# A one-layer transformer block whose last attention groups of each chunk are normalized on the spot by TensorE transposes, with inverse sums and LayerNorm roots from one GpSimd power each

## The chip, the cores and the metric

One core of one Trainium2 chip. The metric is the device time of one execution in microseconds; smaller is better. The kernel before was timed three times: 883.87, 884.46 and 886.01 us, median 884.46 us.

## The reference

A pre-norm transformer block on x of 2048 tokens and 640 features: 32 heads of 20 features, then a gated MLP of width 1728. Weights and data are bfloat16.

```python
def _A_ref(x, wqkv, wo):                       # S = 2048, D = 640, H = 32, Dh = 20
    qkv = (x @ wqkv).reshape(B, S, 3, H, Dh).transpose(2, 0, 3, 1, 4)
    q, k, v = qkv[0], qkv[1], qkv[2]
    scores = jnp.einsum("bhqd,bhkd->bhqk", q, k) * (Dh ** -0.5)
    o = jnp.einsum("bhqk,bhkd->bhqd", _softmax(scores, axis=-1), v)
    return o.transpose(0, 2, 1, 3).reshape(B, S, D) @ wo

h = x + _A_ref(_layernorm(x), A_wqkv, A_wo)
g, u = hn @ w_gate, hn @ w_up                  # hn = _layernorm(h)
out = h + (gelu(g) * u) @ w_down
```

## The kernel before

**Planner.** The program is written as a list of operations, each with an engine, an assumed duration, a priority and its dependencies (class Sched, `op`). `schedule` (line 98) plays that list through once when the program is built and fixes, for each of the five engines, one order of instructions; `emit` (line 263) writes these orders with semaphore waits. Nothing is reordered on the chip: each engine takes its instructions in that order, and a wait holds everything behind it on its engine. A smaller priority number goes first. When PE would be idle, the planner puts in filler matmuls on kt_all and on a zero tile (lines 187 to 227), which compute nothing that is used.

**Tiling.** The 2048 query tokens are cut into eight chunks of 512, 256, 256, 256, 256, 256, 128 and 128 (SIZES). The heads form eight groups of four. A slot is as many groups of one chunk as make 512 columns, so there are 32 slots: eight for chunk 0, four for each of chunks 1 to 5, two for chunks 6 and 7. A slot has 64 score tiles of 128 keys by 512 columns.

**Scores and probabilities.** `unit` issues the score matmuls of two or three tiles (line 976) into PSUM banks 0 to 2 or 3 and 4, and one ACT exponential over 1024 or 1536 columns writes the probabilities to a ring (tiles pts, and pts2 inside rege). D_SLOT says how many quads of tiles per slot do not go to ACT: `d_exp` computes them on VectorE (an eviction at line 889, then four integer operations as terms of an approximate exponential). `pv_op` multiplies the probabilities with the values and a column of ones into bank 6, so that row 20 of each head's 32 rows holds the sum of exponentials.

**Normalization.** At a slot's end `epilogue` copies bank 6 to osb. In chunks 0 to 6 it then calls `spread`: the sums go to DRAM and come back as 128x16 (rc), GpSimd inverts them by a bit trick and three Newton steps (ten operations on rn and rc), the inverses go to DRAM and are broadcast to 128 partitions (bsum), VectorE multiplies (on16), and the rows go to DRAM (attn). All of these transfers are issued on SP. Only chunk 7, the last, is normalized without DRAM: four transposes of osb (line 1063), a reciprocal (line 1069) and scalings into o_nat (line 1072).

**The background work.** After the last slot of a chunk, `post` loads that chunk's attention rows from DRAM into oT, does the output projection (chain, line 676 in 32-column pieces or 681) with the residual (line 1124), LayerNorm (`ln_stats`, `ln_rsqrt`, `ln_apply`), transposes the rows by DMA (for chunk 7 on PE, line 622), and runs gate, up and down matmuls (lines 676 and 1158; 676 and 1223). `ln_rsqrt` computes the root on GpSimd by a bit trick and two Newton steps in 14 operations, then a VectorE reciprocal. This work fills PE between the scores of the next chunk's slots. The width 1728 is cut into 14 tiles of 128 features, the last of which overlaps its neighbour.

**The prologue.** LayerNorm of x, transposes, key, query and value projections. A bound of each score's size is made from the largest absolute key per feature (ka, kd, sel) and added to the queries, so the exponentials cannot overflow. The first scores wait for that bound of head group 0 (`proj_k`, `q_bound0`, lines 793 and 797).

Of the kernel before, what the change touches and what calls it, by code (L numbers as in the profile page):

```python
# [8 lines left out]
ALU = mybir.AluOpType  # L9
# [9 lines left out]
DRAIN = {"pe": 0.165, "act": 0.115, "dve": 0.085, "pool": 0.05, "sp": 0.0}  # L19
WARM_WIN, WARM_MIN = 3.4, 0.5  # L20
PAD_WIN, PAD_MIN = 3.4, 0.42
QK_LEAD = .65
PE_AGE = 3.5
SD_AGE = 0.6
SD_ROW = 0
# [24 lines left out]
class Sched:  # L50
# [47 lines left out]
    def schedule(self):  # L98
# [22 lines left out]
        due = None  # L121
        total = len(ops)
        scores = sum(o.eng == "pe" and o.mode == "row" for o in ops)
        while done < total:
            assert events, "no operation can start"
            t = heapq.heappop(events)
            while events and events[0] <= t + 1e-9:
                heapq.heappop(events)
            for e in ENGINES:
# [8 lines left out]
                while ready[e]:  # L138
# [18 lines left out]
                    if got and 0 < p[0] < 1 and scores > 1 and t - o.ready < (  # L157
                            SD_AGE if mode[e] != "row" else SD_ROW if row_end[o.rows[0]] > max([row_start + 0.01] + [freed[b] for b in got]) + 0.02 else 0):
                        skipped.append((p, i))
                        continue  # L160
# [7 lines left out]
                    if chosen is None:  # L168
                        chosen, banks = o, got
                        if e != "pe" or p[0] < 1 or o.mode == mode[e] or t - o.ready > PE_AGE:  # L170
                            break
# [39 lines left out]
                scores -= o.eng == "pe" and o.mode == "row"  # L211
                if e == "pe" and self.pad is not None and o.tag and o.tag[0] in ("O", "Oq"):
# [21 lines left out]
                if e == "act":  # L234
                    due = t + o.dur + (0.905 if o.dur > 1.2 else 1.332) - QK_LEAD if o.mode == "exp" else None
# [7 lines left out]
                o.fin = t + o.dur + o.lat  # L243
                heapq.heappush(events, free[e])
# [16 lines left out]
        self.span = max(o.fin for o in ops)  # L261
# [63 lines left out]
S = 2048  # L325
# [11 lines left out]
F0 = tuple(min(128 * f, DFF - 128) for f in range(NF))  # L337
SCALE = DH ** -0.5
# [9 lines left out]
PV_QUADS = 2  # L348
PR, PR2 = 12, 4
D_SLOT = (0,) + (3,) * 27 + (2, 3, 2, 1)  # L350
SUMS = (0,) + (1,) * 6 + (0, 1, 1, 0) + (1,) * 5 + (2,) + (1,) * 10 + (0, 1, 1, 1, 0)
# [4 lines left out]
VN = 6  # L356
D_RING = (6,) * 26 + (4, 6, 12, 12, 0, 6)
D_FIRST, D_SPAN = 0, 18
# [5 lines left out]
P_EV = 1.8  # L364
P_QK, P_PV, P_TAIL, P_PRO, P_EPI, P_LN, P_BG = 0, 1, 1.2, 1.5, 2, 2.5, 3
P_KQ = 3
P_ON = 2.4
V_ACT = (0, 1)
XN_DVE = (9, 13, 15)
V0 = 0  # L370
# [3 lines left out]
def bass_sequential_preLN__mha_block__glu_gated_geglu__prompt_kernel(  # L374
# [12 lines left out]
    with ExitStack() as es:  # L387
# [21 lines left out]
        identf = sb("identf", [128, 128], FP32)  # L409
# [13 lines left out]
        kd = sb("kd", [128, NA], FP32)  # L423
        kt_all = sb("kt_all", [128, NG, S])
# [9 lines left out]
        o_nat = sb("o_nat", [128, 1, D])  # L434
# [41 lines left out]
        ob = carve(2 * D).rearrange("p (i s) -> p i s", i=2)  # L476
        I16 = mybir.dt.int16
        ka = carve(2048)
        pts2 = carve(PR2 * 512)
        qreg = [qt_all[:, c, :, :].rearrange("p g s -> p (g s)") for c in range(2)]  # L480
        d_any = [(carve(2048).bitcast(I16), ("da", 0))]
        d_early = [(ha_f[:, 2048 * i:2048 * i + 2048].bitcast(I16), ("dh", i)) for i in range(3)]
# [32 lines left out]
        cst(I("memset", zer[:], 0.0), "zer", 32)  # L515
        op("act", I("activation", nm[:, 0:1], zer[:, 0:2].bitcast(FP32), ACT.Sqrt), 1.5, P_QK, reads=["zer"], writes=["nm0"])
# [21 lines left out]
        for j in range(4):  # L538
            cst(I("memset", off0[32 * j:32 * j + 1, :], OFF), "off0", 1)
        cst(I("memset", identf[:], 0.0), "identf")  # L540
        cst(I("affine_select", out=identf[:], in_=identf[:], compare_op=ALU.not_equal, fill=1.0,
              base=0, pattern=[[-1, 128]], channel_multiplier=1), "identf")
# [36 lines left out]
        def ln_rsqrt(t0, n, prio, table=False, sqrt=False):  # L579
# [7 lines left out]
            d = v if table or sqrt else lambda fn, r, w: op(POOL, fn, 0.285, prio, reads=r, writes=w)  # L587
# [7 lines left out]
            if table:  # L595
                op("act", I("activation", sd16[:, t0:t0 + n], sd16[:, t0:t0 + n], ACT.Sqrt), 0.2, -1, mode="sqrt", reads=[ks],
                   writes=[ks])
                v(I("reciprocal", y, sd16[:, t0:t0 + n]), [ks], rk)
                return
# [724 lines left out]
```

## Time and profile before

| | |
|---|---|
| median of three runs | 884.46 us |
| profiled execution, its own time | 884.74 us |
| its span, first to last instruction | 883.0 us |
| PE, DVE, ACT, POOL busy | 830.0, 753.4, 832.0, 134.2 us |
| first exponential starts, last one ends | 37.02, 842.06 us |
| granted TensorE clock | 1.00 in every stage |

PE is TensorE's matmuls and PEld its weight loads, DVE is VectorE, ACT is ScalarE, POOL is GpSimd, and SP issues DMAs. In the views, "out<-in" gives tile names; rege and regw are two large regions that hold many tiles one after another, so that a name like rege<-ps can mean several things, which the line number tells apart: many operations share line 395. Matmuls that work on separate 32-column or 32-row parts of the array overlap, four to a group, so a row "x60" of such matmuls is 15 groups. PE's busy time counts overlapping matmuls once. In the chain of waits a piece reads start, length, engine and line, and the count of instructions merged in it.

### The profile page before, as it was taken

Reading aid. Unit: us, or ns where it says so; the run is one execution under the profiler, and the core shown is the slowest. Engines: PE = TensorE matmul, PEld = TensorE weight load, DVE = VectorE, ACT = ScalarE, POOL = GpSimd, SP = SyncE. Lnnn points to the kernel's source line nnn. Section 1 sums busy time; section 2 is a strip of 40 time slices with the busy share of each in tenths; the row PEclk is TensorE's granted clock in tenths of the full one; section 3 lists DMA queues with packets and bytes.
Section 4 is the critical chain, followed back from the end, with each engine's and each line's share of the span. In section 5 each row is a group of like instructions: output and inputs, shape, how many; then the busy total and the mean of one; then the engine's idle time right before and its main releaser. Section 6 shows DMA issues by size and latency. Waiting matters only on the chain.

```text
span 883.0 us, 36651 instructions
## 1 busy us (share of the span) xinstructions
PE 830.0 (94%) x16658; PEld 405.4 (46%) x16658; DVE 753.4 (85%) x1356; ACT 832.0 (94%) x798; POOL 134.2 (15%) x431
## 2 busy tenths in 40 slices
PE   3999999999989899999999999999999999999998
PEld 1532222222234333344545555545554556666687
DVE  8839999999879889788899878999899997976864
ACT  6799999999999999999999999999999999999931
POOL 5001111110201201111031211113101321120200
PEclk9999999999999999999999999999999999999999
DMA  7211130332264410001121101101020101103000
GB/s 268 75 44 58 31 79 19 107 90 68 76 175 126 106 30 19 19 8 42 42 64 35 33 17 50 34 8 35 27 57 20 30 19 42 45 16 65 6 17 24
DMA packets 57298, 46.95 MB, mean 53 GB/s; under 512 B 25524, under 2 KB 50704, under 8 KB 57144
## 3 DMA queue, kind: packets, MB, share of 16 engines
q1 hardware_dynamic: 57144, 44.62, 19.2%
q8 instruction: 130, 2.13, 1.0%
q14 instruction: 24, 0.20, 0.1%
HBM read 30.68 MB, written 11.04 MB: 47 GB/s over the span
## 4 chain that ended last, share of the span: by engine, by line
ACT 56%; PE 28%; DVE 12%; POOL 1%; issue 1%; DMA 1%
ACT pts L395 44%; ACT rege L395 12%; PE ps L676 9%; PE ps L976 7%; PE ps L395 5%; PE ps L681 4%; DVE qt_all L395 3%; DVE rege L889 2%; PE ps L1158 2%; DVE rege L395 2%; DVE qt_all L889 1%; DVE stats L395 1%; PE ps L1223 1%; DMA rege<-xn_t 1%; ACT qt_all L395 1%
## 5 line engine op out<-in xcount | busy, mean ns | idle before, releaser
L395 ACT ACTIVATE pts<-ps 128x1024 bf16<-128x1024 f32 (+1 forms) x585 | 639.3, 1244 | 8.0 <-PE ps L976 6.1
L976 PE MATMUL ps<-qt_all,kt_all 32*128 32x256 bf16 (+2 forms) x4096 | 301.2, 272 | 24.3 <-ACT pts L395 17.5
L976 PEld LDWEIGHTS ps<-qt_all,kt_all 32*128 32x128 bf16 x4096 | 101.8, 92 | 227.1 <-ACT pts L395 150.5
L395 ACT ACTIVATE rege<-ps 128x1536 bf16<-128x1536 f32 (+1 forms) x129 | 178.6, 1401 | 1.7 <-PE ps L395 1.5
L889 DVE TENSOR_SCALAR rege<-ps 128x512 int16<-128x512 f32 x220 | 148.7, 682 | 27.9 <-PE ps L976 27.2
L676 PE MATMUL ps<-rege,regw 128*32 128x256 bf16 (+1 forms) x3360 | 152.4, 292 | 5.7 <-ACT rege L395 1.8
L395 PE MATMUL ps<-pts,v_all 128*21 128x256 bf16 (+2 forms) x2711 | 132.1, 273 | 0.3 <-ACT pts L395 0.2
L395 PE MATMUL ps<-rege,v_all 128*21 128x256 bf16 (+2 forms) x1877 | 130.1, 287 | 2.3 <-issue 1.5
L889 DVE TENSOR_SCALAR qt_all<-ps 128x512 int16<-128x512 f32 x136 | 92.2, 683 | 19.7 <-PE ps L976 18.8
L676 PEld LDWEIGHTS ps<-rege,regw 128*32 128x32 bf16 x3360 | 77.9, 96 | 44.5 <-issue 24.9
L395 DVE TENSOR_SCALAR rege<-rege 128x2048 int16<-128x2048 int16 x139 | 93.3, 684 | 2.5 <-PE ps L395 1.9
L681 PE MATMUL ps<-regw 128*128 128x512 bf16 (+1 forms) x360 | 90.2, 356 | 2.5 <-ACT regw L628 2.0
L395 POOL TENSOR_SCALAR rn<-rc 128x16 int32<-128x16 int32 x30 | 8.6, 288 | 526.2 <-DMA rc<-sums 525.8
L395 PEld LDWEIGHTS ps<-pts,v_all 128*21 128x21 bf16 x2711 | 62.4, 91 | 30.1 <-issue 23.3
L676 PE MATMUL ps<-regw,rege 128*32 128x320 bf16 x1568 | 74.7, 301 | 0.6 <-DVE rege L889 0.5
L395 DVE TENSOR_SCALAR qt_all<-qt_all 128x2048 int16<-128x2048 int16 (+2 forms) x118 | 68.8, 594 | 0.6
L395 PEld LDWEIGHTS ps<-rege,v_all 128*21 128x21 bf16 x1877 | 50.1, 91 | 36.4 <-issue 20.9
L395 PE MATMUL ps<-qt_all,v_all 128*21 128x256 bf16 (+1 forms) x1360 | 58.8, 262 | 0.5 <-DVE qt_all L395 0.3
L395 DVE TENSOR_SCALAR qt_all<-rege 128x2048 int16<-128x2048 int16 x83 | 56.2, 689 | 1.6 <-PE ps L395 1.0
L681 PEld LDWEIGHTS ps<-regw 128*128 128x128 bf16 x360 | 29.3, 99 | 51.1 <-issue 26.6
L1211 DVE TENSOR_TENSOR rege<-rege,ps 128x512 bf16<-128x512 bf16 (+1 forms) x53 | 35.8, 677 | 12.1 <-PE ps L676 11.2
L676 PEld LDWEIGHTS ps<-regw,rege 128*32 128x32 bf16 x1568 | 36.6, 96 | 19.0 <-issue 9.3
(113 smaller groups left out, 724.2 us busy)
## 6 DMA issues: line engine op xcount, KB each, us to landing
bsum<-rsums SPq DMA_DIRECT2D x120, 64.0 KB, 2.1
rege<-in_A_x_dram SPq DMA_DIRECT2D x5, 640.0 KB, 5.6
q_rows<-regw SPq DMA_DIRECT2D x20, 128.0 KB, 1.8
out_dram<-rege SPq DMA_DIRECT2D x16, 160.0 KB, 2.6
attn<-on SPq DMA_DIRECT2D x120, 20.0 KB
regw<-in_B_w_gate_dram SPq DMA_DIRECT2D x5, 432.0 KB, 3.6
regw<-in_B_w_up_dram SPq DMA_DIRECT2D x5, 432.0 KB, 3.3
kt_all<-k_rows SPq DMA_DIRECT2D x12, 160.0 KB
```

The lines of the kernel that those rows point to most:

```text
L395: return lambda eng: getattr(eng, method)(*args, **kwargs)
L676: return [lambda eng, j=j: eng.matmul(out()[32 * j:32 * j + 32], l[:, 32 * j:32 * j + 32], r, start=start, stop=stop, tile_position=(0, 32 ...
L681: fn = col4(lambda: bank(bk, n), l, r, k == 0, k == len(steps) - 1) if col else lambda eng, l=l, r=r, k=k: eng.matmul(bank(bk, n), l, r, s ...
L889: d_ops.append(op("dve", lambda eng: eng.tensor_scalar(v[:, 512 * h:512 * h + 512], bank(b), EXP_MUL, -32000.0, ALU.mult, ALU.max), c_dve( ...
L976: return lambda eng: eng.matmul(out()[:, kk * nq:(kk + 1) * nq], kt_all[32 * j:32 * j + 32, g, kt * 128:(kt + 1) * 128], qt_all[32 * j:32 ...
L1158: lambda eng, a=a, f=f, fi=fi: eng.matmul(bank(bk)[:, fi * nq:(fi + 1) * nq], w[:, a, F0[f]:F0[f] + 128], hnT[:, a, 128 * tb:128 * tb + nq ...
L1211: hdone.append(op("dve", lambda eng, bu=bu, fv=fv, w=w: eng.tensor_tensor(fv, fv, bank(bu, w), ALU.mult), c_dve(w), p, reads=[ku] + hkeys( ...
L1223: f == NF - 1) if nq >= COL else lambda eng, f=f, o=o, hf=hf, bk=bk: eng.matmul(
```

## The change

1. *Direct normalization.* In chunks 0 to 6 the last slot (in chunk 0 the last two) is no longer sent through `spread`. Four TensorE transposes, a VectorE reciprocal and scalings put the normalized rows in a small buffer (wda or sq), and small 32-column matmuls with the identity turn them back into oT. The oT load from DRAM carries only the other slots' rows, in two DMAs.
2. *Powers.* The inverse of the sums is one GpSimd power with exponent -1, the LayerNorm root one power with exponent 0.5.
3. *Prologue.* The largest absolute key of head group 0 is reduced by VectorE with an absolute-value reduction (three of four from SBUF, the last one from PSUM). Values wait for it from the fourth tile on.
4. *Last feature tile.* 1728 = 13 x 128 + 64. Where the chunk has 256 or 512 tokens, the last tile's 64 features are laid out as two halves of the tokens, so these matmuls stream half the columns; a second copy of the last w_down rows (wda) serves the first half.
5. *Output.* The last addition is written over h_sb instead of a separate buffer.
6. *Planner.* Several constants become tuples by slot, background work gets new priorities, PV matmuls go in one quad at a time (PV_QUADS 2 to 1), the probability ring grows from 16 to 19 tiles, D_SLOT, SUMS, D_RING and D_SPAN change by slot, chunk 3's LayerNorm rows are transposed on PE (XP_PE), and ACT's assumed pace gets 12 ns per instruction more.

```diff
-DRAIN = {"pe": 0.165, "act": 0.115, "dve": 0.085, "pool": 0.05, "sp": 0.0}
+DRAIN = {"pe": 0.165, "act": 0.118, "dve": 0.085, "pool": 0.05, "sp": 0.0}
-QK_LEAD = .65
-PE_AGE = 3.5
+QK_LEAD = (0.65, 0.55,) + (0.65,) * 4 + (0.72, 0.72, 0.6,) + (0.72,) * 8 + (0.6, 0.6, 0.72, 0.6,) + (0.68,) * 11
+ACT_GAP = .012
+PE_AGE = (2.5,) * 9 + (1.5, 2.5, 2.5, 5.0,) + (1.0,) * 7 + (5.0,) + (1.0,) * 5 + (3.5, 2.0, 2.0, 1.0, 3.5, 1.0,)
...
-PV_QUADS = 2
-PR, PR2 = 12, 4
-D_SLOT = (0,) + (3,) * 27 + (2, 3, 2, 1)
+PV_QUADS = 1
+PR, PR2 = 13, 6
+D_SLOT = (0,) + (3,) * 3 + (2,) + (3,) * 3 + (4,) + (3,) * 19 + (2, 3, 0, 1,)
...
-P_EV = 1.8
+P_EV = 1.5
-P_KQ = 3
+P_KQ = (2, 3, 3, 3)
+X_LAT = 3.0
+O_LAT = 3.2
+XP_PE = (3,)
+P_NOW = 0.9
+PW = 0.4
+P_K0 = 1.0
+P_DV = 0.5
+P_ADD = 0.6
+P_ST = 0.7
+P_OUT = 2.5
...
@@ ln_rsqrt @@
+            if not dve:
+                op(POOL, I("tensor_tensor", sd16[:, t0:t0 + n], sd16[:, t0:t0 + n], rn[:, 1, 0:n], ALU.pow), PW, prio,
+                   reads=[ks, "pwc"], writes=[ks])
                 v(I("reciprocal", y, sd16[:, t0:t0 + n]), [ks], rk)
                 return
...
@@ proj_qk @@
+            if dkey[0] == "ku" and t == 0:
+                red = lambda src, r: op("dve", lambda eng: eng.tensor_reduce(km[:, c:c + 1], src(), AX.X, ALU.max, apply_absolute_value=True),
+                                        0.62, P_K0, reads=[r], writes=[("km", c)])
+                m = [red(lambda: bank(bk), key)] if c == 3 else []
...
@@ spread @@
-            x, y, z = rc[:, s, :], rn[:, 0, :], rn[:, 1, :]
-            d = lambda fn, r, w: op(POOL, fn, 0.285, P_EPI, reads=r, writes=w)
-            d(I("tensor_scalar", y.bitcast(I32), x.bitcast(I32), -1.0, RECIP_MAGIC, ALU.mult, ALU.add), [("rc", s)], ["ry"])
-            for i in range(3):
-                d(I("tensor_tensor", z, x, y, ALU.mult), [("rc", s), "ry"], ["rz"])
-                d(I("tensor_scalar", z, z, -1.0, 2.0, ALU.mult, ALU.add), ["rz"], ["rz"])
-                d(I("tensor_tensor", x if i == 2 else y, y, z, ALU.mult), ["ry", "rz"], [("rc", s) if i == 2 else "ry"])
+            op(POOL, I("tensor_tensor", rc[:, s, :], rc[:, s, :], rn[:, 0, :], ALU.pow), PW, P_EPI, reads=[("rc", s), "pwc"],
+               writes=[("rc", s)])
...
@@ epilogue @@
-            if c < len(CHUNKS) - 1:
+            tail = c == len(CHUNKS) - 1
+            g_dir = [g for ss, (cc, gg) in enumerate(slots) if cc == c and (tail or gg[-1] == NG - 1 or c == 0 and gg[0] == NG - 2)
+                     for g in gg]
+            if gs[0] not in g_dir:
                 spread(s, c, gs, nq)
                 return
...
+            op("sp", I("dma_start", oT[:, 0:na, tok], src[0:128 * na, :].rearrange("(a p) s -> p a s", p=128)), 0.4, P_EPI,
+               reads=ars, writes=hk, sem=f"oT{c}", lat=O_LAT + nq * 0.004, after=tuple(e_ops) if c == 0 else ())
+            op("sp", I("dma_start", oT[0:pf, na, tok], src[128 * na:f0, :]), 0.4, P_EPI,
+               reads=ars, writes=hk, sem=f"oT{c}", lat=O_LAT + nq * 0.004, after=tuple(e_ops) if c == 0 else ())
...
+                        fs = [lambda eng, i=i, a=a, tt=tt, q=q, b3=b3: eng.matmul(
+                            bank(b3)[q:q + 32, i * nq + tt * 128:i * nq + tt * 128 + 128],
+                            buf[:, tt, 128 * a + q - f0:128 * a + q - f0 + 32], ident[:], start=True, stop=True,
+                            tile_position=(0, q), skip_group_check=True) for q in range(p0, 128, 32)]
+                        op("pe", fs, 0.057, P_NOW, mode="col", util=0.03, reads=[okey(0, tt), "ident"], writes=[k3],
+                           acq=[b3] if i == 0 and tt == 0 else [], after=free if i == 0 and tt == 0 else ())
...
@@ post @@
-            if not tail:
-                op("sp", I("dma_start", oT[:, :, 128 * tb:128 * tb + nq],
-                           adr[c].rearrange("g j e s -> (g j e) s").rearrange("(a p) s -> p a s", p=128)), 0.4, P_EPI,
-                   reads=[("adr", c, gs[0], j) for cc, gs in slots if cc == c for j in range(4)],
-                   writes=[("hnT", tt) for tt in range(tb, tb + nt)], sem=f"oT{c}", lat=4.5 + nq * 0.002, after=first)
...
+                    half = nq >= COL and f == NF - 1
...
+                        fn = [lambda eng, a=a, fi=fi, j=j: eng.matmul(
+                            bank(bk)[32 * j:32 * j + 32, fi * nq:fi * nq + nq // 2], w[:, a, FL + 32 * (j % 2):FL + 32 * (j % 2) + 32],
+                            hnT[:, a, 128 * tb + j // 2 * (nq // 2):128 * tb + (j // 2 + 1) * (nq // 2)], start=a == 0, stop=a == NA - 1,
+                            tile_position=(0, 32 * j), skip_group_check=True) for j in range(4)] if half else col4(lambda fi=fi: bank(bk)[:, fi * nq:(fi + 1) * nq], w[:, a, F0[f]:F0[f] + 128],
```

220 lines of the change are left out of this document (144 added, 76 removed).

## The prediction

> **What bounds the kernel now.** I read the page's totals and chain of waits first, then busy time by stage, then the order in time around the first exponential, one chunk's end, and the end of the run.
>
> ```profile
> span 883.0 us, 36651 instructions
> ACT 56%; PE 28%; DVE 12%; POOL 1%; issue 1%; DMA 1%
> ACT pts L395 44%; ACT rege L395 12%; PE ps L676 9%; PE ps L976 7%; PE ps L395 5%; PE ps L681 4%; DVE qt_all L395 3%; DVE rege L889 2%; PE ps L1158 2%; DVE rege L395 2%; DVE qt_all L889 1%; DVE stats L395 1%; PE ps L1223 1%; DMA rege<-xn_t 1%; ACT qt_all L395 1%
> ```
>
> More than half of the chain is ACT writing probabilities (pts, and the rege copies of that ring). PE follows with background work (L676 is MLP and output projection). One engine does not bound everything, so I split the span where the first exponential starts and the last one ends (us, then busy time of PE, PEld, DVE, ACT, POOL with instruction counts, clock, DMA share, GB/s):
>
> ```profile
> 0.00:37.00 37.00, 22.08 (x154) 12.34 (x154) 30.51 (x96) 24.60 (x45) 12.17 (x32) 1.00 0.52 176
> 37.00:212.00 175.00, 171.43 (x1458) 51.35 (x1457) 148.29 (x261) 173.85 (x161) 19.67 (x60) 1.00 0.24 64
> 212.00:305.00 93.00, 84.81 (x1409) 32.16 (x1405) 80.83 (x142) 93.00 (x87) 15.89 (x55) 1.00 0.45 121
> 305.00:730.00 425.00, 406.74 (x9224) 204.62 (x9228) 383.21 (x647) 423.77 (x394) 70.97 (x226) 1.00 0.13 31
> 730.00:842.00 112.00, 107.44 (x3734) 73.39 (x3726) 87.68 (x161) 108.14 (x102) 15.52 (x58) 1.00 0.16 35
> 842.00:883.00 41.00, 37.53 (x704) 31.51 (x695) 22.83 (x52) 8.61 (x14) 0.00 (x0) 1.00 0.05 18
> ```
>
> Three stages with three limits. Up to 37 us a prologue; from 37 to 842 ACT is busy 173.85 + 93.00 + 423.77 + 108.14 = 798.76 of 805 us, so 6.2 us idle; from 842 on ACT is done and PE is busy 37.53 of 41 us. That last stage is what the change can shorten most, so I ask what PE does there (start, us, work):
>
> ```profile
> 840.10 0.33 PE ps L976 x4
> 840.98 1.42 PE ps L676 x50
> ...
> 849.93 6.77 PE ps L676 x196
> ...
> 861.22 6.90 PE ps L1158 x119
> 868.12 3.81 PE ps L1223 x28
> 871.92 3.75 PE ps L1158 x67
> ...
> 875.70 0.43 DVE rege L1183
> ...
> 876.18 3.99 PE ps L1223 x28
> ```
>
> At 840.10 the last score matmuls run; PE then works almost without a break to 880.17, 40 us. L676 there is chunk 5's MLP, half of L1158 and the first L1223 are chunk 6's: a backlog. The last chunk's own chain queues behind it. Why the backlog exists shows at a chunk's end: its last sums are copied, and the output projection (wo) starts only when sums, inverses, broadcasts and rows have gone through DRAM:
>
> ```profile
> 730.19 0.69 DVE L395 COPY osb<-ps 128x512 f32<-128x512 f32 x1 [1.45 <-PE ps L395]
> 750.66 0.68 DVE L395 TENSOR_TENSOR on<-osb,bsum 128x512 bf16<-128x512 f32 x1
> 763.44 1.09 PE L676 MATMUL ps<-wo,rege 128*32 128x320 bf16 x20
> 831.09 0.27 POOL L395 CAST mv<-mv 128x2 bf16<-128x2 f32 x1 [37.29 <-DVE mv L395]
> 836.36 0.19 POOL L395 TENSOR_TENSOR sd<-nw,rs 128x1 bf16<-128x1 f32 x1
> ```
>
> Chunk 5: 33 us from copy to projection. The last two rows are the ends of chunk 6's root on GpSimd, 14 operations in 5.5 us.
>
> **The change part by part.** Counts come from the two programs' instruction orders; durations from rows.
>
> *Tail.* After the last score matmul the old order holds 140 matmuls of 32x256, 224 of 32x320, 280 of 128x128, 56 of 128x320. The new one holds no 32x256 and no 32x320, 210 of 128x128, 56 of 128x320 and 20 fillers. Moved into the exponential stage: 35 groups of four at 1.42/12.5 = 0.114 us, 56 groups at 6.77/49 = 0.138 us and 70 singles at 6.90/119 = 0.058 us: 4.0 + 7.7 + 4.1 = 15.8 us. What remains on PE is about 24 us, less than the last chunk's own chain, so that chain now ends the run:
>
> ```profile
> 841.39 0.67 ACT L395 ACTIVATE pts<-ps 128x512 bf16<-128x512 f32 x1
> 842.85 0.68 DVE L395 COPY osb<-ps 128x512 f32<-128x512 f32 x1
> 845.34 0.66 PE L1063 MATMUL ps<-identf,osb 128*128 128x128 f32 x4
> 852.66 0.45 DVE L395 TENSOR_SCALAR xn_t<-rege,mu,rs 128x640 bf16<-128x640 bf16 x1
> 856.63 0.45 PE L622 MATMUL ps<-ident,xn_t 128*128 128x128 bf16 x5
> 857.12 0.70 ACT L628 ACTIVATE rege<-ps 128x640 bf16<-128x640 bf16 x1 [3.35 <-PE ps L622]
> 880.19 0.49 DVE L1228 TENSOR_TENSOR rege<-ps,rege 128x320 bf16<-128x320 f32 x1 [1.34 <-PE ps L1223]
> ```
>
> From the last exponential's end (842.06) to the copy 0.8. From copy to the end of xn_t 853.11 - 842.85 = 10.3, less 1.6 that the transposes waited behind L676 (copy over at 843.53, transposes at 845.34), plus 1.1 for two DVE multiplies (0.69 and 0.42, a 512 and a 256 wide L1211) that the new order puts into it: 9.8. Transposes and their eviction, 856.63 to 857.82, and a step: 1.4. Gate and up, 140 x 0.058 = 8.1; the last multiply 0.5; down 4.0; 880.19 to the end 2.8. Sum 27.4, against 883.0 - 842.06 = 40.9: 13.5 us less. The two multiplies may find their place elsewhere: 14.6 at best; if the two waits on PE stay as now, 13.5 - 1.6 - 3.5 (853.11 to 856.63) = 8.4.
>
> *First exponential.* The abs and maximum steps on key projections become reductions straight from PSUM.
>
> ```profile
> 31.55 0.60 ACT L708 ACTIVATE regw<-ps 128x512 bf16<-128x512 f32 x1 [0.48 <-PE ps L681]
> 34.67 0.24 DVE L395 TENSOR_SCALAR sel<-sel,kd 128x4 bf16<-128x4 bf16 x1
> 34.97 0.39 PE L793 MATMUL ps<-regw,sel 128*128 128x512 bf16 x1
> 37.02 1.45 ACT L395 ACTIVATE pts<-ps 128x1536 bf16<-128x1536 f32 x1 [3.58 <-PE ps L976]
> ```
>
> From the last key eviction to sel now takes 3.1 us; one reduction of 512 (a 512-wide DVE read of PSUM is 0.68, the copy above), a small one and sel make 1.2. But PE, in its fixed order, still has other projections ahead of L793: in all 25 instead of 30 V matmuls of 320 come before the first scores. So the gain is what PE drops, 5 x 0.138 = 0.7 plus some of a short wait: 0.9, between 0 and the 1.9 of the DVE chain.
>
> *ACT's work.* D_SLOT gives 2 quads (8 tiles) back to ACT: two-bank exponentials 448 to 443, three-bank 265 to 271. Their pitch, from the chain:
>
> ```profile
> 96.03 5.01 ACT pts L395 x5
> 101.03 1.34 ACT rege L395
> ```
>
> Five rows of which one is three-bank: (5.01 - 1.34)/4 = 0.917, and 1.34. So 6 x 1.34 - 5 x 0.917 = +3.5. By the same rows 512 columns cost 0.42. Shorter GELUs (the last feature tile is now half) drop 896 columns, 0.7; one 1024-wide tanh, about one two-bank step, moves out of the tail into the stage, +0.9: +3.7 in all. The planner's other new constants (ACT_GAP, QK_LEAD, PE_AGE, SD_AGE by slot) only set the order, which the counts hold already.
>
> *PE in the stage.* In: 15.8 us, and 1 us of small transposes and 32-wide matmuls per boundary, 6-7. Out: the halved last feature tile, 40 groups of 256 columns and 10 of 512 at half their length, 40 x 0.057 + 10 x 0.114 = 3.4; fillers (matmuls on kt_all and zer, with no use but activity) from 114 groups of 512 columns to 69, 45 x 0.228 = 10.3. Net about +9 in 805 us. What makes room is the time at the boundaries: chunk 5's and 6's projection can start about 25 us earlier. So I let ACT's idle time stay at 6.2 us; bounds: all of it goes (-6.2), or all moved work comes back as ACT waiting (+15.8).
>
> *GpSimd.* 30 chains of ten operations become 22 single powers, and the roots shrink from 14 to 4 operations. No row shows a power. The nearest, a two-operand 128x16 operation, is 0.35; the far end is a whole chain:
>
> ```profile
> L395 POOL TENSOR_TENSOR rn<-rc,rn 128x16 f32<-128x16 f32 x90 | 31.6, 352 | 6.7
> 711.78 1.09 POOL L395 TENSOR_SCALAR rn<-rc 128x16 int32<-128x16 int32 x1 [16.76 <-DMA rc<-sums]
> 718.09 0.22 POOL L395 TENSOR_TENSOR rc<-rn 128x16 f32<-128x16 f32 x1
> DVE rs L395 <- POOL sd L395: 1.5, 4, 0.4
> ```
>
> 0.35 to 6.5 us; I take 0.35, same engine, shape and operands. At that, POOL stays off the path. The last row is the wait that the power lengthens if slow: DVE's reciprocal, with score evictions (L889) behind it in DVE's queue and the gate matmuls behind the normalised rows in PE's.
>
> *The rest at no cost.* Eight slots skip the DRAM trip (82 of 519 SP transfers go; attn rows now move for 22 slots), the oT load is split in two on SP and waits for earlier slots only; DVE trades eight 0.68 multiplies and eight score evictions of the same length for reciprocals, small scalings and evictions, no more work than before, covered by ACT. A weight copy (wda) and a late identity load on idle POOL and SP. If DVE's cover fails, the new evictions delay the projection, not ACT.
>
> *A rule against it.* The clock column above reads 1.00 in every stage. The Trainium skill, "TensorE: Matmul & The Clock Gate", Part 1, says that PE falls to half its clock after an idle window of about 3.4 us; this change removes 45 filler groups. No row here shows such a fall.
>
> **The sum.** -0.9 + 3.7 - 13.5 + 0 = -10.7 against the profiled execution's own 884.74 (span 883.0 and 1.7 around it); the median, 884.46, is 0.3 below it. 884.46 - 10.7 = 873.8.
>
> **The rivals.**
> - *More:* ACT's idle time goes too, and the tail gives 14.6: 873.8 - 6.2 - 1.1 = 866.5. For it: shorter boundary chains; against: ACT has been idle under 1% anyway. 0.13.
> - *The backlog comes back as ACT waiting.* PE is busy 107.44 of 112 us from 730 on, and takes more work in. Fully: 873.8 + 15.8 = 889.6; half: 881.7; slower than before from 10.7/15.8 = 68% on. Against: fillers and a 25 us earlier start. 0.10.
> - *The power is slow* (the other side): place, the seven roots. PE's order is fixed and was laid out for a short root; each microsecond over 0.4 holds the gate matmuls and the scores behind them, up to seven times. It decides from 10.7/7 + 0.4 = 1.9 us; at 3 us, half a chain, 7 x 2.6 = 18.2: 892.0. For: unshown operation. Against: the old root shown took 5.5 us where 13 steps of 0.285 were planned, and PE lived with it. 0.09.
> - *PE clock falls* between 212 and 305, where fillers lie thickest (44 groups, 10 us): 84.81 - 10 = 75 us of work at half speed is 150, +57 over the 93: 931. Against: real work replaces the fillers. 0.02. (This is what the rule of the Trainium skill above would do.)
>
> **How the numbers follow.** Forecast 0.66 (its own range 867 to 880: tail 8.4 to 14.6, start 0 to 1.9, a few us of idle time), rivals 0.13, 0.10, 0.09, 0.02. The range 862 to 885 takes in "more" with room, half of the second rival, and leaves the slow power and the clock out. About 0.3% (2.7 us) is what a measurement of this kernel can tell from no change. Faster: 0.65 + 0.13 + 0.05 = 0.83; same: 0.01 + 0.02 + 0.02 = 0.05; slower: 0.03 + 0.07 + 0.02 = 0.12.
>
> **What would show it.** Right: first exponential near 36 us; last one near 845; then about 27 us in which PE has gaps and no 32-row matmuls; wo within 10 us of a chunk's last copy; a power row of 0.3 to 0.6 us. Wrong: ACT idle above 15 us between (backlog), gaps of PE ending at POOL or at rs (power), a clock under 1.00, or a tail still above 35 us.

## The result, and the profile after

The changed kernel takes 880.24 us (median of five runs, 876.74 to 881.07) against 884.28 us for the kernel before on the same chip: a ratio of 0.994, interval 0.992 to 0.996. Run once more beside the last experiment it took 878.52 us, ratio 0.9925 (0.9912 to 0.9939). It is faster, as forecast, but by 4.0 us in the first series and 7.4 us in the second, where 10.7 us were forecast. The profiled execution of the first series (881.07 us) has a span of 879.4 us; its totals and its chain of waits:

```profile
span 879.4 us, 36235 instructions
PE 839.4 (95%) x16663; PEld 409.0 (47%) x16663; DVE 749.1 (85%) x1369; ACT 839.7 (95%) x800; POOL 94.3 (11%) x85
PE 49%; ACT 30%; DVE 14%; DMA 4%; issue 1%; POOL 1%; SPq 1%; DVEq 0%
```

ACT held 56% of the chain before and PE 28%; now PE holds 49%. (A name that ends in q is that engine's sequencer.) The busy time by stage, in the same columns as before:

```profile
37.00:212.00 175.00, 171.25 (x1406) 51.98 (x1405) 144.35 (x252) 174.61 (x161) 18.63 (x7) 1.00 0.24 63
212.00:305.00 93.00, 89.44 (x1474) 36.28 (x1475) 86.05 (x156) 89.66 (x84) 10.31 (x8) 1.00 0.39 99
305.00:730.00 425.00, 415.71 (x9503) 211.62 (x9502) 391.74 (x676) 422.15 (x390) 48.14 (x29) 1.00 0.12 31
730.00:845.00 115.00, 111.26 (x3680) 72.86 (x3676) 79.38 (x157) 112.30 (x103) 5.33 (x9) 1.00 0.10 24
```

PE is busy 787.7 of these 808 us; before it was 770.4 of 805. ACT's busy time here adds up to 798.72 of 808 us, so 9.3 us idle; before it was 6.2. The clock stays at 1.00. The end of the run in order of time (some of its rows):

```profile
850.65 1.50 ACT L428 ACTIVATE rege<-ps 128x1024 bf16<-128x1024 f32 x2
852.66 0.69 DVE L428 COPY osb<-ps 128x512 f32<-128x512 f32 x1
861.45 0.45 DVE L428 TENSOR_SCALAR xn_t<-rege,mu,rs 128x640 bf16<-128x640 bf16 x1
862.06 0.44 PE L660 MATMUL ps<-ident,xn_t 128*128 128x128 bf16 x5
863.70 7.98 PE L1243 MATMUL ps<-rege,regw 128*128 128x128 bf16 x140
872.19 3.98 PE L1311 MATMUL ps<-regw,rege 128*128 128x320 bf16 x28 [0.52 <-DVE rege L1269]
876.21 0.49 DVE L1316 TENSOR_TENSOR rege<-ps,rege 128x320 bf16<-128x320 f32 x1 [1.41 <-PE ps L1311]
```

The first row merges the last two exponentials, which end at 852.15 (850.65 + 1.50); the tail after them is 27.25 us (879.4 - 852.15), where 27.4 were forecast. No 32-row MLP matmul is left in it. The first exponential starts at 35.97, where about 36.1 was forecast. So the whole miss lies between the two: the exponential stage takes 816.2 us, where 805.0 + 3.7 = 808.7 was forecast.

**Where the stage's time went.** From now on three numbers describe a run: the stage (first exponential's start to last one's end), the tail (from there to the end of the span) and the waits. The waits are a sum over all exponentials of two or three banks: from its start to the start of ACT's next instruction, less the shortest such pitch, which is 0.903 us for two banks and 1.330 us for three. It is 19.0 us before and 26.5 us after; the difference, 7.6 us before rounding, is the miss. ACT's idle time in the view above grew by only 3.1 us, because an exponential's record is longer than the step to the next one's start (1.06 us for two banks, whose shortest step is 0.903): a wait shorter than that overlap leaves no idle time.

```profile
L428 ACT ACTIVATE pts<-ps 128x1024 bf16<-128x1024 f32 x294 | 301.9, 1061 | 1.9 <-PE ps L1026 1.5
```

Sorted by size, waits of 20 to 640 ns, nearly all of them ended by score matmuls (L976, now L1026), grew from 12.1 us to 19.2 us. The few above 640 ns were 4.7 us (four) and are 4.2 us (two). So the growth as a whole is in many short waits for scores, while among the long ones a new one has taken the place of others. That new one is 3.06 us (some rows of the time around it):

```profile
255.81 5.54 ACT L428 ACTIVATE pts<-ps 128x1024 bf16<-128x1024 f32 x5
262.32 0.39 PE L428 MATMUL ps<-kt_all 128*128 128x512 bf16 x1
262.43 0.68 DVE L428 TENSOR_SCALAR rege<-qt_all 128x2048 int16<-128x2048 int16 x1
263.34 0.40 PE L428 MATMUL ps<-kt_all,zer 128*32 128x512 bf16 x4
263.57 0.61 PE L428 MATMUL ps<-rege,v_all 128*21 128x256 bf16 x16
264.23 1.94 ACT L428 ACTIVATE rege<-ps 128x1024 bf16<-128x1024 f32 x2 [2.89 <-PE ps L428]
```

The busy time between 255 and 264 us, in the columns of the stages:

```profile
255.00:264.00 9.00, 8.27 (x163) 3.67 (x159) 8.94 (x15) 6.34 (x6) 1.62 (x2) 1.00 0.33 94
```

ACT stops at 261.34 and waits 2.89 us for a PV matmul that frees its place in the probability ring. That PV comes in PE's fixed order after PV matmuls on VectorE's approximate tiles, and VectorE is busy 8.94 of 9.00 us: this is slot 8, where D_SLOT gives VectorE four quads instead of three, and where VectorE also evicts chunk 0's directly normalized rows (L1160, at 257.66 and 259.29). PE is not what is short here, since it runs fillers (kt_all, zer) in the gap.

The other term is the power. In all groups of GpSimd's operations, it stands with its real price:

```profile
L428 POOL TENSOR_TENSOR rc<-rc,rn 128x16 f32<-128x16 f32 x22 | 68.7, 3124 | 406.9 <-DMA rc<-sums 406.9
L428 POOL TENSOR_TENSOR sd<-sd,rn 128x2 bf16<-128x2 bf16 (+2 forms) x7 | 6.6, 944 | 0.0
```

It takes 3.12 us for the sums and 0.94 us for the roots, where the prediction took 0.35 and the planner (PW) 0.4. The old ten operations took 4.12 us from first to last, as a mean over the 30 slots. Around 300 us the chain of waits runs through two powers and the DRAM trips behind them (start, length, piece):

```profile
297.62 3.66 DMA rc<-sums
301.36 3.44 POOL rc L428
304.82 2.29 DMA rsums<-rc
308.42 2.88 DMA bsum<-rsums
311.40 0.69 DVE on L428
...
318.62 3.29 POOL rc L428
321.94 1.38 DMA rsums<-rc
324.63 3.58 DMA bsum<-rsums
328.23 0.69 DVE on L428
330.72 0.40 PE ps L428 x8
331.92 1.45 ACT pts L428
```

VectorE stands in its fixed order at "on", the multiply with bsum, until the broadcast lands; PE and then ACT (1.15 us of waiting ahead of 331.92) come after it.

### The profile page after: what moved, and what is told of

Read it like the earlier page. It is cut to its first block, busy times and chain, and to the rows that moved or that the text cites. A ratio compares the mean times of both kernels' runs of the same rounds, so it can differ in the third digit from the quotient of the medians.

```text
span 879.4 us, 36235 instructions
## 1 busy us (share of the span) xinstructions
PE 839.4 (95%) x16663; PEld 409.0 (47%) x16663; DVE 749.1 (85%) x1369; ACT 839.7 (95%) x800; POOL 94.3 (11%) x85
## 4 chain that ended last, share of the span: by engine, by line
PE 49%; ACT 30%; DVE 14%; DMA 4%; issue 1%; POOL 1%; SPq 1%; DVEq 0%
ACT pts L428 20%; PE ps L1026 15%; PE ps L719 12%; PE ps L428 12%; ACT rege L428 9%; PE ps L724 6%; DVE qt_all L428 3%; DVE rege L428 2%; DVE rege L939 2%; PE ps L1243 2%; DVE qt_all L939 2%; DMA regw<-in_A_wqkv_dram 1%; PE ps L1311 1%; SPq L428 1%; POOL rc L428 1%
## 5 line engine op out<-in xcount | busy, mean ns | idle before, releaser
L428 ACT ACTIVATE pts<-ps 128x1536 bf16<-128x1536 f32 (+1 forms) x494 | 557.0, 1233 | 5.4 <-PE ps L1026 4.5
L1026 PE MATMUL ps<-qt_all,kt_all 32*128 32x256 bf16 (+2 forms) x4096 | 316.7, 272 | 9.1 <-ACT pts L428 3.3
L428 ACT ACTIVATE rege<-ps 128x1024 bf16<-128x1024 f32 (+2 forms) x221 | 249.1, 1193 | 4.9 <-PE ps L428 2.9
L1026 PEld LDWEIGHTS ps<-qt_all,kt_all 32*128 32x128 bf16 x4096 | 109.0, 92 | 206.8 <-issue 75.7
L719 PE MATMUL ps<-rege,regw 128*32 128x256 bf16 (+1 forms) x3120 | 146.1, 292 | 4.4 <-DVE rege L939 1.1
L428 PE MATMUL ps<-pts,v_all 128*21 128x256 bf16 (+2 forms) x2392 | 142.1, 274 | 0.9 <-DVE osb L428 0.9
L428 PE MATMUL ps<-rege,v_all 128*21 128x256 bf16 (+2 forms) x2204 | 136.9, 285 | 1.9 <-issue 0.6
L428 POOL TENSOR_TENSOR rc<-rc,rn 128x16 f32<-128x16 f32 x22 | 68.7, 3124 | 406.9 <-DMA rc<-sums 406.9
L428 PEld LDWEIGHTS ps<-pts,v_all 128*21 128x21 bf16 x2392 | 49.7, 90 | 48.1 <-issue 40.7
L1297 DVE TENSOR_TENSOR rege<-rege,ps 128x512 bf16<-128x512 bf16 (+2 forms) x53 | 34.8, 657 | 8.8 <-PE ps L719 7.6
```

The costliest lines, as they stand in the source:

```text
L428: return lambda eng: getattr(eng, method)(*args, **kwargs)
L719: return [lambda eng, j=j: eng.matmul(out()[32 * j:32 * j + 32], l[:, 32 * j:32 * j + 32], r, start=start, stop=stop, tile_position=(0, 32 ...
L1026: return lambda eng: eng.matmul(out()[:, kk * nq:(kk + 1) * nq], kt_all[32 * j:32 * j + 32, g, kt * 128:(kt + 1) * 128], qt_all[32 * j:32 ...
L1297: hdone.append(op("dve", lambda eng, bu=bu, fv=fv, w=w: eng.tensor_tensor(fv, fv, bank(bu, w), ALU.mult), c_dve(w), p, reads=[ku] + hkeys( ...
```

## The experiments

All runs by the three numbers; ratios are to the kernel before on the same chip. Stage, tail and waits are of the profiled execution; two profiles of the changed kernel differ by 2 us in the stage.

```
run                              median   ratio [95%]              stage  tail  waits
before                           884.28   1                        805.0  40.9  19.0
changed                          880.24   0.994  [0.992, 0.996]    816.2  27.3  26.5
e12 changed again                878.52   0.9925 [0.9912, 0.9939]  814.1  27.2  24.5
e1  multiply for power           877.64   0.9904 [0.9887, 0.9922]  813.3  27.3  23.6
e2  three powers                 934.72   1.0552 [1.0513, 1.0592]  875.9  27.2  86.3
e9  control: new order           886.75   1.0016 [1.0007, 1.0026]  823.0  28.8  33.4
e3  slot 8: three quads          886.89   1.0006 [0.9992, 1.002]   814.0  34.6  23.5
e4  two quads of PV              886.40   1.0005 [0.9994, 1.0016]  818.1  31.5  29.4
e5  rows through DRAM            889.75   1.0051 [1.0037, 1.0065]  820.8  33.9  32.0
e6  full last tile               891.03   1.0071 [1.0056, 1.0086]  822.6  31.4  33.1
e7  true power price             882.50   0.9968 [0.9957, 0.9979]  813.9  31.3  25.2
e8  before with powers           889.92   1.0062 [1.0042, 1.0082]  812.1  40.1  26.0
e10 before, powers, same order   883.80   0.9988 [0.9976, 1.0]     805.0  40.9  19.0
e11 true price, new constants    874.56   0.9873 [0.9857, 0.9889]  810.8  27.0  21.1
```

**The power's price in a fixed order.** Two runs keep every engine's order and change only what GpSimd issues in it.

```diff
-op(POOL, I("tensor_tensor", rc[:, s, :], rc[:, s, :], rn[:, 0, :], ALU.pow), PW, P_EPI, ...
+op(POOL, I("tensor_tensor", rc[:, s, :], rc[:, s, :], zer[:].bitcast(FP32), ALU.mult), PW, P_EPI, ...
...
-op(POOL, I("tensor_tensor", sd16[:, t0:t0 + n], sd16[:, t0:t0 + n], rn[:, 1, 0:n], ALU.pow), PW, prio, ...
+op(POOL, I("tensor_tensor", sd16[:, t0:t0 + n], sd16[:, t0:t0 + n], rn[:, 1, 0:n], ALU.mult), PW, prio, ...
```

> The changed kernel's order of instructions on every engine, but each GpSimd power is a plain multiply of the same shape (the sums by zero, the roots by 0.5): inverse sums and roots are left out, so 22 slots' attention rows are zero. The power rows should fall from 3.12 us and about 1.0 us to some 0.35 us. Power theory (the seven missing microseconds are waits behind 3.12 us powers in an order laid out for 0.4): the last exponential moves from 850.6 us towards 844.8, the total from 880.2 to about 873 to 875. Slot-8 theory (one fixed stall of 3.06 us at 260 us) and full-PE theory (TensorE has no room in the exponential stage): last exponential within 1.5 us of 850.6, the 3.06 us stall still at 260, total 878.5 to 880.5.

```diff
-op(POOL, I("tensor_tensor", rc[:, s, :], rc[:, s, :], rn[:, 0, :], ALU.pow), PW, P_EPI, ...
+op(POOL, [I("tensor_tensor", pwx[:, i, :], rc[:, s, :], rn[:, 0, :], ALU.pow) for i in (0, 1)] + [
+    I("tensor_tensor", rc[:, s, :], rc[:, s, :], rn[:, 0, :], ALU.pow)], PW, P_EPI, ...
```

> The same order again, with three powers in place of one for each of the 22 inverse sums (two go to a scratch tile): 3.12 us becomes about 9.4 us per slot. Power theory: if 2.7 us too much per power cost 7 us in all, 6.2 us more cost at least another 10: total above 890. Slot-8 and full-PE theories: below 2 us more, about 880 to 882, since the sums' way through DRAM has time to spare.

The GpSimd row of e1:

```profile
L428 POOL TENSOR_TENSOR rc<-rc,zer 128x16 f32<-128x16 f32 x22 | 6.5, 295 | 447.3 <-DMA rc<-sums 447.3
```

From each run's waits, the row in which SP, whose queue issues the DMAs, waits for the inverse sums (us in total, times, longest), for e1, then the changed kernel, then e2:

```profile
SPq L428 <- POOL rc L428: 33.4, 18, 4.1
```

```profile
SPq L428 <- POOL rc L428: 86.6, 21, 6.3
```

```profile
SPq L428 <- POOL rc L428: 221.6, 22, 13.4
```

And e2 in order of time, SP's and PE's instructions around one of these waits:

```profile
140.73 0.34 SPq L428 DMA_DIRECT2D rsums<-rc  x1
144.79 0.59 SPq L428 DMA_DIRECT2D qt_all<-bounds  x1
...
146.87 0.61 PE L1027 MATMUL ps<-qt_all,kt_all 32*128 32x512 bf16 x2 [4.16 <-DMA qt_all<-bounds]
```

A multiply of 0.30 us in the power's place takes 2.9 us off the waits of the first series' profile and 0.9 off the second's; by the ratios (0.9904 against 0.994 and 0.9925) it is worth 2 to 3 us, with intervals that touch that of the first series and overlap that of the second. 877.64 us lies between what the power theory and the two others expected. So the price costs about 1 to 3 of the 7.6 us, near what can be told from nothing, and not all of it; the 3.04 us wait in slot 8 is still there in e1. But the price is not off the path: at 9.4 us the run is 54 us longer, a part of which is a granted clock of 0.965 on average (see the last section). These rows show the way: SP issues in order, the inverse's DMA (rsums) holds the transfers behind it, and at 146.87 the scores have waited 4.16 us for query bounds that were issued late. The slot-8 and full-PE theories, which expected less than 2 us more, fail on e2.

**The control.** Every other edit lays the order out anew, so one run measures what a new order alone costs.

```diff
-D_LAT = 0.3
+D_LAT = 0.31
```

> A control: the changed kernel with one assumed latency of the planner moved from 0.30 to 0.31 us (D_LAT, how early a VectorE tile's scores are placed before its slot needs them); the same instructions and counts, but every order is laid out anew. It tells what a new order alone costs, against which the edits of one constant or one part are to be read. Tuned-order theory (the constants by slot fit this one order, and any other is worse): 3 to 9 us above 880.2, with waits spread over many places, so that most of what three quads, two quads, rows through DRAM and the full last tile lost is the new order and not the edit. Edit theory (those losses are the edits' own): 880 to 882.

The same instructions in a new order cost 0.76% (1.0016 against 0.994), some 6.7 us, as the theory expected by which the constants by slot fit one order. It is one new order; how far others spread was not measured. The 3.09 us wait of slot 8 is there too, and others of 2.45 and 1.32 us are new. So e3 to e7 are read against 1.0016 as well as against the changed kernel.

**Slot 8 with three quads.**

```diff
-D_SLOT = (0,) + (3,) * 3 + (2,) + (3,) * 3 + (4,) + (3,) * 19 + (2, 3, 0, 1,)
+D_SLOT = (0,) + (3,) * 3 + (2,) + (3,) * 3 + (3,) + (3,) * 19 + (2, 3, 0, 1,)
```

> D_SLOT of slot 8 from 4 quads back to 3, order laid out anew. Slot-8 theory: four quads (16 tiles) make VectorE late in that slot, PV matmuls in their fixed order wait for its last tile, and ACT waits for a ring slot. With 3 the 3.06 us stall at 260 falls under 0.5 us, ACT gets four tiles more (4 x 0.42 = 1.7 us), and the last exponential moves by -3.06 + 1.7 = -1.4 to about 849. Full-PE theory: the stall also goes, but what TensorE did in it is now missing, so it comes back as other waits or as a longer tail: total 880 or more, up to 885. Power theory: the stall stays.

The wait is gone (no wait above 0.5 us between 250 and 280), and the stage is 814.0 us: 2.2 less than in the first profile, and the same as in e12. But the tail is 34.6 us. What PE does in it:

```profile
855.76 1.52 PE L724 MATMUL ps<-wo,rege 128*128 128x320 bf16 x10
859.87 3.91 PE L1243 MATMUL ps<-rege,regw 128*128 128x128 bf16 x67 [2.58 <-DVE rege L428]
864.75 3.98 PE L1311 MATMUL ps<-regw,rege 128*128 128x320 bf16 x28 [0.52 <-DVE rege L1297]
868.56 7.98 PE L1243 MATMUL ps<-rege,regw 128*128 128x128 bf16 x140
877.06 3.98 PE L1311 MATMUL ps<-regw,rege 128*128 128x320 bf16 x28 [0.52 <-DVE rege L1269]
```

67 gate and up matmuls and 28 down matmuls of chunk 6 stand behind the last chunk's projection and before its own 140. So without the fourth quad the wait does not arise, and taking it away alone gains nothing: the order that results leaves chunk 6 for the tail. But the quad is not the whole cause, as e5 and e11 below show.

**Two quads of PV at a time.** PV rows' busy time in the stage is 334 us after against 321 before, for no more matmuls, and PV_QUADS went from 2 to 1.

```diff
-PV_QUADS = 1
+PV_QUADS = 2
```

> PV_QUADS from 1 back to 2: PV matmuls go in runs of 16 instead of 8, order laid out anew. Full-PE theory with short runs (a run of 8 takes 0.40 us, one of 16 takes 0.62, and the changed kernel holds 567 PV runs in the stage against 431): PV rows' busy time falls from 334 to some 321 us, TensorE's busy share of the stage falls, ACT's excess wait of 26.5 us falls by several us. If run length is only bookkeeping, PV busy falls as well but ACT's waiting does not, and the later probabilities could make it longer (slot 8 above all): total 880 to 890. Power theory: no change.

PV's busy time falls to 307 us, and PE's busy time between 37 and 845 does not (786.6 against 787.7 us), nor do ACT's waits. Run length is no cost that can be seen here, as far as a new order lets one see it; nothing speaks for the shorter PV runs as the cause of the miss.

**Direct normalization and the halved tile taken out.**

```diff
-            if gs[0] not in g_dir:
+            if not tail:
                 spread(s, c, gs, nq)
+                if gs[-1] == NG - 1:
+                    op("sp", I("dma_start", oT[:, :, 128 * b0:128 * b0 + nq], ...
```

> Direct normalization taken out of chunks 0 to 6: their last slots go through DRAM like the others, one oT load per chunk, as in the kernel before; all else as in the changed kernel, order laid out anew. Full-PE theory (the stage has no room on TensorE, and the shorter tail comes from work that the direct path lets start earlier): chunk 6's MLP is late again, the tail after the last exponential grows from 27.5 us to 33 us or more, while the exponential stage becomes a few us shorter, since some 12 us of small transposes go and the work starts later: last exponential at 846 to 849, total 882 to 888. If instead the direct path costs nothing in the stage, the stage stays at 814.7 us and the total rises by the whole growth of the tail, to 886 or more. If it brings nothing, the total is 880.

```diff
-                    half = nq >= COL and f == NF - 1
+                    half = False
...
-                return min(512, (NF - k * fn_) * nq - (nq // 2 if nq >= COL else 0))
+                return min(512, (NF - k * fn_) * nq)
```

> The last feature tile at full length again (no halves) for chunks of 256 and 512 tokens, order laid out anew. It puts 40 x 0.057 + 10 x 0.114 = 3.4 us of matmuls back on TensorE in the stage. Full-PE theory: this comes back almost one for one, as ACT waiting or as tail: total 882 to 886, stage plus tail longer by 2 to 6 us. If TensorE had room: total 880 to 881.

Without the direct path the tail is 33.9 us, 5.1 longer than the control's, and the run 0.35% slower than the control, about 3 us. That the stage would get shorter was wrong against the changed kernel: 820.8 us against 816.2, though the control has 823.0. The full tile costs 0.55% against the control, 4.9 us for an edit of some 3 us of PE time, and 891.03 us is more than either theory expected. Both differences are smaller than the 6.7 us that a new order alone cost, so that the two parts earn something is likely but not shown, and how much of the 14 us tail gain is the direct path's cannot be told from these runs.

One thing e5 does show: it keeps slot 8's four quads, and between 235 and 285 us none of its waits is above 0.25 us, with VectorE as busy as in the changed kernel (8.82 of 9.00 us):

```profile
255.00:264.00 9.00, 8.29 (x158) 3.31 (x154) 8.82 (x15) 9.00 (x10) 0.00 (x0) 1.00 0.63 186
```

So the wait of slot 8 is absent without the fourth quad (e3) and without the direct path (e5); every other new order of the changed kernel with both at the fitted constants has 2.7 to 4.1 us of it (e4, e6, e7, control). As far as these orders show, it needs both, and an order that brings them together.

**The plan's price of a power.**

```diff
-PW = 0.4
+PW = 3.1
...
-                op(POOL, I("tensor_tensor", sd16[:, t0:t0 + n], sd16[:, t0:t0 + n], rn[:, 1, 0:n], ALU.pow), PW, prio,
+                op(POOL, I("tensor_tensor", sd16[:, t0:t0 + n], sd16[:, t0:t0 + n], rn[:, 1, 0:n], ALU.pow), 1.0, prio,
```

> The planner's price of a power raised to what the trace shows: 3.1 us for the sums, 1.0 us for the roots (0.4 before for both), order laid out anew; the same computation. Power theory: what the cheap multiply won in the fixed order (about 3 us, half of it between 300 and 350 us) is won back, since nothing is placed ahead of its data any more: the stage falls from 814.7 to about 812 us, total 877 to 879. Full-PE theory: the stage gets shorter by 1 to 3 us, but the later start of the projections costs as much in the tail: total 880 to 884.

Two more runs put the powers into the kernel before: once laid out anew at 0.4 us, once in the old order of every engine.

```diff
-            x, y, z = rc[:, s, :], rn[:, 0, :], rn[:, 1, :]
...
+            op(POOL, I("tensor_tensor", rc[:, s, :], rc[:, s, :], rn[:, 0, :], ALU.pow), 0.4, P_EPI, reads=[("rc", s), "pwc"],
+               writes=[("rc", s)])
```

> The kernel before with the powers alone (inverse sums and roots, planned at 0.4 us each), order laid out anew. The power takes 3.12 us where the ten operations took 4.12 (mean), so in itself it is no loss on GpSimd; what can hurt is that the plan now counts on 0.4 instead of 2.85. Power theory: 30 powers too late by 2.7 us each in TensorE's fixed order cost 2 to 4 us: 886 to 888. If the old order's slack at the chunk ends (33 us from copy to projection) covers it: 883 to 885, no difference.

```diff
+        self.order = [o for o in self.order if o.i not in self.drop]
...
+            one(n0, I("tensor_tensor", x, x, rn[:, 0, :], ALU.pow))
```

> The kernel before in its own order on every engine, laid out with the ten and fourteen GpSimd operations of old, but issuing one power in the place of each chain (30 inverse sums, 7 roots; the dropped operations take no time). The power's 3.12 us stands where the chain took 4.12 us (mean) and was planned at 3.7. Price theory (the power is harmless in itself; it hurts only where the plan counts on 0.4): 883 to 885, between 0 and 2 us below the kernel before, against 889.9 when the same powers are planned at 0.4. If a power were harmful in another way: 886 or more.

In e10 the old order stays on all engines, and the power that replaces the ten operations is worth 0.12%, at the edge of nothing. Planned at 0.4 us, the same powers in the kernel before cost 0.62%, some 5 us, more than either theory expected, and the waits go from 19.0 to 26.0 us: part or all of that may be the new order, as in the control. With its true price in the plan the changed kernel's new order (e7) is 0.5% better than the control's new order, but 0.3 to 0.4% worse than the fitted one, by its tail of 31.3 us; 882.50 us is what the full-PE theory expected and not the 877 to 879 us of the power theory.

**Both together.** The true prices again (3.1 and 1.0 us), and the constants by slot fitted anew to them (QK_LEAD, PE_AGE, SD_AGE, SD_ROW, SUMS, D_RING, D_SPAN); D_SLOT stays as it was, so slot 8 keeps four quads.

```diff
-PW = 0.4
+PW = 3.1
...
-QK_LEAD = (0.65, 0.55,) + (0.65,) * 4 + ...
+QK_LEAD = (0.78, 0.55, 0.6, 0.55, 0.78, 0.72, 0.5, 0.5, 0.65, ...)
...
-SUMS = (0,) + (1,) * 7 + (0, 1, 0,) + ...
+SUMS = (2, 1, 1, 0, 1, 2, 0, 1, 0, 1, 2, ...)
...
```

> The same computation with the power planned at 3.1 and 1.0 us, and the planner's constants by slot (D_SLOT, SUMS, QK_LEAD, PE_AGE, SD_AGE, SD_ROW, D_RING, D_SPAN) chosen anew for an order with that price; slot 8 keeps its four quads. Price-and-order theory (the missing microseconds are an order laid out for the wrong price and the stall in slot 8, not a lack of room on TensorE as such): the stall at 260 falls under 1 us, the stage from 815.7 to 810 to 813 us with the tail still 27 to 29 us, total 874 to 878, below the changed kernel (880.2) and the kernel before. Full-PE theory in its strict form (what is saved as waiting comes back as tail, microsecond for microsecond): 879 to 882.

> The changed kernel once more, unchanged, on the same chip as the run with new constants, so that the two can be compared directly and the runs of different days against each other: ratio to the kernel before 0.992 to 0.996, the 3.06 us stall at 260 again, stage 815 to 816 us, tail 27 to 28 us.

The new constants give 874.56 us, ratio 0.9873 against 0.9925 on the same chip: faster than both kernels. e12's stage, 814.1 us, is a microsecond shorter than expected; its wait in slot 8 is 3.05 us. The largest wait around slot 8 is 0.73 us, and the waits sum to 21.1 us, near those of the kernel before, with all the moved work in the stage and a tail of 27.0 us. ACT's exponentials over the place of the old wait:

```profile
255.57 3.05 ACT L428 ACTIVATE rege<-ps 128x1024 bf16<-128x1024 f32 x3
259.23 5.54 ACT L428 ACTIVATE pts<-ps 128x1536 bf16<-128x1536 f32 x5 [0.61 <-PE ps L1026]
```

This decides against the strict form of the full-PE theory, that PE has no room: busy 787.5 of 808 us between 37 and 845, as in the changed kernel, it carries the same work with 3.4 us less waiting than e12. The short waits of 20 to 640 ns are 13.7 us in it, against 12.1 us before and 17.3 in e12. How much of the 4.0 us between e11 and e12 comes from the price and how much from fitting again stays open: no run fits the constants again at 0.4 us.

## Why the prediction was right in its sign and short in its size

The forecast was 873.8 us; the measured 880.24 lies at the upper edge of the forecast's own range (867 to 880) and inside 862 to 885. The sign came from the tail, as the prediction said.

- **Tail, -13.5 us: right.** 27.25 us against 27.4. The order of the end was also as described: the last chunk's own chain ends the run, and its terms hold one by one (from copy to the end of xn_t 9.2 us for 9.8, gate and up 7.98 for 8.1, down 3.98 for 4.0).
- **First exponential, -0.9 us: right.** 35.97 against 37.02. But in the four runs of the same order (changed, e12, e1, e2) it lies between 34.9 and 36.0, and in the two of the old order at 36.3 and 37.0 (e10, before), so that the first profile hits -0.9 so closely is luck.
- **ACT's work, +3.7 us: right.** The counts are 443 and 271, and 805.0 + 3.7 + 7.6 of waits = 816.3, against a stage of 816.2.
- **ACT's idle time, 0: this is the step that failed.** The prediction let ACT's idle time stay at 6.2 us, since fewer fillers and an earlier projection would make room on PE. The waits grew by 7.6 us (5.5 in the second profile). The term was also read in a view that shows only a part: 6.2 of the 19.0 us of waits before, and 9.3 of the 26.5 after. The long wait of slot 8 stands in three runs of this order (3.06, 3.04, 3.05): the prediction counted D_SLOT's quads in sum, and did not ask whether VectorE could deliver a fourth one in the very slot that also holds chunk 0's direct path. The power is 1 to 3 us. The short waits for scores grew by 7.2 us, of which the power is a part; e11 brings most of this back at the same work, so the amount of work does not force them, but no run takes them apart further.
- **GpSimd, 0.35 us: wrong, within its bounds (0.35 to 6.5).** It is 3.12 us. "At that, POOL stays off the path" fell with it. The rival that named a slow power put it at the roots, which take only 0.94 us; it enters at the sums. The rows point to SP's order and VectorE's multiply with bsum as the way.
- **PE in the stage, +9 us: too small.** PE's busy time rose by 17 us up to 845, and by 25 us up to the last exponential (795.3 us between 36 and 852, against 770.4). Small transposes and 32-wide matmuls take 11.8 us in the stage (lines 1116, 1153 and 660) instead of 6 to 7, and busy time of unchanged work rose too. The row of the 256-column scores in the stage, before and after:

```profile
L976 PE MATMUL ps<-qt_all,kt_all 32*128 32x256 bf16 x2560 | 185.8, 273 | 20.7 <-ACT pts L395 15.4 <-ACT rege L395 3.2 <-DVE rege L1211 0.4
```

```profile
L1026 PE MATMUL ps<-qt_all,kt_all 32*128 32x256 bf16 x2560 | 198.8, 272 | 5.6 <-ACT pts L428 2.2 <-ACT rege L428 0.8 <-DVE rege L939 0.7
```

The same 2560 matmuls: PE waited 18.6 us for ACT ahead of them, now 3.0. Busy and idle together are about the same, 206.5 and 204.4, and one matmul takes as long as before (273 and 272 ns), so they overlap less. Most of PE's slack against ACT ahead of these scores is gone, so a late tile or row can now reach ACT; that the short waits come from this is a reading of the rows, which no run tests by itself.
- **Projection 25 us earlier: half right.** Chunk 5's copy and its projection, after:

```profile
738.89 0.68 DVE L428 COPY osb<-ps 128x512 f32<-128x512 f32 x1
...
751.08 0.73 PE L719 MATMUL ps<-wo,rege 128*32 128x320 bf16 x16
```

12.2 us from copy to projection instead of 33, though not within 10; in the run it comes 12 us earlier than before.
- **Rivals.** "The backlog comes back" at half gives 881.7, close to what was measured, and ACT does wait for scores in many short pieces as it says; but by e11 the moved work as such does not force these waits. "More" (866.5) did not come.
- **The clock: did not fall** here, with 45 filler groups fewer.

## What to carry to other kernels

An operation that no row shows should be timed by itself before a static order is laid out with it: 0.4 us assumed for 3.12 us cost about 1 to 3 us here, and 54 us more once it was three times as long in the same order. In a kernel whose order was fitted constant by constant, an edit is judged against a control with a new order and no edit, which here cost 6.7 us, more than either part of the change that was taken out. Where work moves from the critical engine to a second one, look at what else that engine has to do in that very slot. Its busy share does not tell: VectorE was busy 8.94 of 9.00 us where ACT stood, and 8.82 in e5 where ACT did not wait. And idle time in a table of busy times misses waits that are shorter than the overlap of two instructions; steps from start to start show them.

## What was not expected of the hardware

GpSimd's power on 128x16 float32 takes 3.12 us (0.30 us for a multiply of the same shape), so nearly all of it is the function and not the instruction.

The clock falls after quite short gaps of PE. In e2 PE stood for 4.16 us before 146.87, and in the control for 2.43 us before 300.24 (busy times and clock in the columns of the stages; e2 first):

```profile
143.00:147.00 4.00, 0.13 (x2) 0.13 (x2) 0.48 (x1) 1.06 (x1) 0.00 (x0) 0.87 0.35 92
147.00:151.00 4.00, 3.75 (x21) 1.07 (x19) 3.90 (x7) 1.65 (x2) 0.00 (x0) 0.50 0.08 21
```

```profile
300.00:310.00 10.00, 9.76 (x168) 3.73 (x172) 6.19 (x10) 7.59 (x7) 0.00 (x0) 0.83 0.41 121
```

A mean of 0.83 over 10 us is 3.4 us at half speed. The length of one gap does not decide: the control's clock also fell after a gap of 1.21 us (before 283.11), and the kernel before has a gap of 1.29 us (before 312.86) without a fall.

```profile
283.00:290.00 7.00, 6.68 (x84) 2.18 (x84) 4.54 (x8) 5.74 (x6) 0.00 (x0) 0.76 0.96 167
```

```profile
310.00:318.00 8.00, 6.34 (x126) 2.65 (x124) 5.32 (x10) 6.96 (x8) 2.15 (x10) 1.00 0.24 46
```

The Trainium skill, "TensorE: Matmul & The Clock Gate", Part 1, describes a free-running window of 3413 ns and has the clock at half after at least one idle window. The 3.4 us and the 0.50 agree with it; that a whole window must be idle does not, as the gaps of 2.43 and 1.21 us show. So a stall of PE in this kernel can cost twice: once as the gap, and once as some microseconds at half speed after it. The longest gap of PE that the changed kernel's waits list in the stage is 0.9 us.
